# Two small expert groups of the second layer share their result tiles and scattering products; the first layer's small group scatters in two slices; three maxima over k stand earlier

## The chip, the cores and the metric

The kernel runs on one core of one Trainium2 chip. The time is device time in microseconds (us), from launch to end, and less is better. The engines are TensorE (PE; its weight loads are shown as PEld), VectorE (DVE), ScalarE (ACT), GpSimd (POOL) and SyncE (SP), which issues nearly all DMA transfers. Each engine works through its own instructions in the order in which they were written.

## The reference

Linear attention over 4 batches of 8 heads (576 tokens, 64 features a head), then two mixture-of-experts layers over the 2304 tokens of 512 features:

```python
q_s = exp(q - q.max(-1)); q_s /= q_s.sum(-1) + 1e-9
k_s = exp(k - k.max(2));  k_s /= k_s.sum(2) + 1e-9      # over the tokens
x = einsum('bhsd,bhde->bhse', q_s, einsum('bhsd,bhse->bhde', k_s, v))
...
# first layer: the best of 8 experts for each token, by order of arrival up to a capacity
h = relu(disp @ w1); y = h @ w2                           # 512 -> 1024 -> 512
out[i] = gate_w[i] * y[expert_idx[i], pos[i]]             # 0 where no place is left
# second layer: only tokens with x @ w_skip > 0
out[do_compute] = xc + gate_w * (relu(xc @ w1[e]) @ w2[e])
```

## The kernel before

**Layout.** x stands transposed in SBUF, 512 features as 4 chunks c of 128 partitions, 576 tokens along the free axis, one tile for each batch. A product over tokens is written in two halves of 288 columns.

**Large groups.** `COURSE` lists five large groups (layer, batch): (0,0), (0,1), (0,2), (1,0), (1,1). Each runs one expert over all 576 tokens of a batch, in 16 slices: 8 for the first weight matrix (L842), 8 for the second (L863), with 24 products of 288 columns in each slice. An fp32 operand is split into a high and a low part: `split_w` makes `wh` on ACT and `wl` on DVE (L784, L785), two slices ahead of use, and the slice's result in PSUM (`pair`) is evacuated as `hh` on ACT (L876) and `hl` on DVE (L877).

**The order.** Everything else is hung onto the slices by hand. One line of `COURSE` is one slice: its products, then `split_w` of the slice two ahead, then the words left of the bar, then `evacuate`, then the words right of the bar. Names with c, d, e, f, g, i are half batches of attention (`km`, `kt`, `kc`, `ke`, `kv`, ... are steps of k; `qm`, `q1`, ..., `qt` of q; `re` gives x). `km` takes the maximum of k over the tokens within each partition, three DVE operations (L378 to L380, tile `m`). `kt` transposes that on PE (L386, tile `pt`), so PE waits there for `km`. C and M are steps of the routing, O stores, G steps of the gate row, L and N loads of weights, X splits of x.

**Small groups.** An expert with at most 32 tokens of a batch is done apart: S is (0,2) with one such expert, T is (1,2) with two. The tokens are gathered (`g`), five steps `t` run the expert on 32 places (L1206), and its result in PSUM has four row blocks of 32 partitions: blocks 0 and 1 hold feature chunks 0 and 1, blocks 2 and 3 hold chunks 2 and 3, each pair of blocks the two partial sums over the hidden features. Step 4 splits that into the two tiles `y2` (high and low, L1223, L1224); their other places stay zero. `v` (`places`) compares each token's code with the 32 place codes, four copies side by side (L1228, L1232), and `a` (`place`) transposes that into `pT` (128 rows, 576 tokens). `u` (`put`, L1255 and L1259) scatters: for each chunk and token half two products of `y2[:, c]` with `pT` into a PSUM tile `pts`, and one DVE addition of it to x. Before, `put(t, i)` handles chunks 2i and 2i+1 of expert t: 8 products and 4 additions.

**PSUM.** All the small PSUM tiles (`pts`, `pt`, `ptl`, `px`, `pg`, `pgm`, `pkT`, ...) rotate through the three buffers of one pool, `bank`:

```python
pa = ctx.enter_context(tc.tile_pool(name="pa", bufs=3, space=bass.MemoryType.PSUM))
def bank(name):
    return pa.tile([P, 512], F32, name=name, tag="a")
```

The fourth such tile in a row therefore waits until the first has been read.

Of the kernel before, what the change touches and what calls it, by code (L numbers as in the profile page):

```python
# [9 lines left out]
F32 = mybir.dt.float32  # L10
# [3 lines left out]
ALU = mybir.AluOpType  # L14
# [3 lines left out]
P = 128  # L18
NJ = 5
LAST = 64  # L20
HT = 288
TINY = 32
# [25 lines left out]
    L5 c.q2 | C0.2 c.kc  # L48
    C0.3 c.ke d.qm |
    L6 C0.4 c.q3 | c.kv  # L50
    C0.5 c.qn d.q1 |
    L7 d.km | c.qt d.kt
    C0.6 d.q2 | d.kc
    d.ke | c.re G.0
    d.q3 X0 | d.kv
# [5 lines left out]
    C1.3 e.qm N3 f.ld | C1.4  # L61
    """),
    ((0, 1), """
    L4 C1.5 |
    e.km e.q1 | e.kt
    L5 C1.6 e.q2 | G.3 e.kc
    e.ke f.qm | G.1
    L6 e.q3 | e.kv
    e.qn f.q1 | G.2
    L7 f.km | e.qt f.kt  # L70
    f.q2 | f.kc
    f.ke | e.re
    f.q3 X0 | f.kv
# [20 lines left out]
    N2 g.qn S.v0 | S.t03  # L94
    X2 | S.a0 g.qt
    N3 | S.t04
    X3 | S.u00 S.u01
    """),
    ((1, 0), """
    L4 G.3 | g.rw  # L100
    g.rx | M2.1
    L5 | M2.2 M1.1
    M2.3 | M2.4
# [14 lines left out]
    L4 G.3 | T.t03 O0.2  # L118
    | T.a0 i.rw
    L5 i.rx | T.t04 C3.1  # L120
    T.v1 | T.t10 T.u00
    L6 | T.u01 C3.2 G.1
    C3.3 | T.t11 C3.4 O0.3
    L7 C3.5 G.2 | T.t12 T.a1
    | T.t13
    Z B |
    | T.t14
    | T.u10
    | T.u11 O1.0
    | O2.0  # L130
    | O1.1 O2.1
    | O2.2
# [6 lines left out]
def kernel(  # L139
# [17 lines left out]
    nc = tc.nc  # L157
    B, H, S, D = q.shape
# [23 lines left out]
    def bank(name):  # L182
        return pa.tile([P, 512], F32, name=name, tag="a")

    def long_bank(name):

        return pb.tile([P, 512], F32, name=name, tag="b")
# [17 lines left out]
    def tokens(a):  # L205
        return slice(a * HT, (a + 1) * HT)
# [7 lines left out]
    iota = c32[:, C_IOTA:C_IOTA + TINY]  # L214
# [9 lines left out]
    for i, g in enumerate((w_gate, w_gate2)):  # L224
        t = cp.tile([P, NC, 32], F32, name=f"wg{i}")
        nc.gpsimd.memset(t, 0.0)
        with nc.allow_non_contiguous_dma(reason="gate weights are small"):
            nc.scalar.dma_start(out=t[:, :, 0:E], in_=g.rearrange("(c p) e -> p c e", p=P))
            if i == 1:
                nc.scalar.dma_start(  # L230
                    out=t[:, :, E:E + 1], in_=w_skip.rearrange("(c p o) -> p c o", p=P, o=1)
# [22 lines left out]
    for i in range(2):  # L254
        t = cp.tile([P, 2, P], F32, name=f"kvd{i}")
# [694 lines left out]
    with tc.tile_pool(name="fp", bufs=1) as fp:  # L950
# [3 lines left out]
        a, b = [Half(0, hh, X[0], fp, 1) for hh in range(2)]  # L954
# [158 lines left out]
    hp = ctx.enter_context(tc.tile_pool(name="hp", bufs=1, reuse_waits="tile"))  # L1113
    hp = ctx.enter_context(tc.tile_pool(name="hp", bufs=1, reuse_waits="tile"))
# [7 lines left out]
    class Small:  # L1122
# [69 lines left out]
        def expert(self, t, step):  # L1192
            if step == 0:
                self.ph = long_bank("ph")
            elif step == 3:
                self.ph = long_bank("py")
            if step != 2:
                for i in {0: (0, 1), 1: (2, 3), 3: (4, 5), 4: (6, 7)}[step]:
                    w = self.tw.pop(8 * t + i)
                    for g in range(4):  # L1200
                        if i < 4:
                            lhsT, rhs = self.xs[:, i, 32 * t:32 * t + 32], w[:, 256 * g:256 * g + 256]
                        else:
                            lhsT = self.hT[:, g % 2, 32 * (i - 4):32 * (i - 4) + 32]
                            rhs = w.rearrange("p (u d) -> p u d", u=2)[:, g % 2, 256 * (g // 2):256 * (g // 2) + 256]
                        nc.tensor.matmul(  # L1206
                            out=self.ph[32 * g:32 * g + 32, :256], lhsT=lhsT, rhs=rhs, start=(i % 4 == 0), stop=(i % 4 == 3)
                        )
                    self.load(8 * t + i + 3)
            if step == 1:  # L1210
                self.h1 = hp.tile([P, 256], F32, name="h1", tag="h1")
                nc.scalar.activation(self.h1, self.ph[:, :256], AF.Relu)
            elif step == 2:
                pt = bank("pth")
                for u in range(2):
                    nc.tensor.transpose(pt[:, u * P:(u + 1) * P], self.h1[:, u * P:(u + 1) * P], ident)
                self.hT = hp.tile([P, 2, P], F32, name="hT", tag="h1")
                nc.vector.tensor_copy(out=self.hT, in_=pt[:, :2 * P].rearrange("p (u s) -> p u s", u=2))
            elif step == 4:
                for i in range(2):  # L1220
                    sl, cs = slice(64 * i, 64 * i + 64), slice(2 * i, 2 * i + 2)
                    src = self.ph[sl, :256].rearrange("p (c d) -> p c d", c=2)
                    nc.scalar.copy(y2[0][sl, cs], src)  # L1223
                    nc.vector.tensor_sub(y2[1][sl, cs], src, y2[0][sl, cs].bitcast(F32))  # L1224

        def places(self, t):
            cs = hp.tile([P, TINY], F32, name="cs2", tag="cs2")
            nc.vector.tensor_scalar(out=cs, in0=iota, scalar1=self.r["tlo"][:, t:t + 1], scalar2=None, op0=ALU.add)  # L1228
            self.p4 = hp.tile([P, NJ, 4, TINY], F32, name="p4", tag="ot", bufs=3)
            bb = [P, NJ, TINY]  # L1230
            for g in range(4):
                nc.vector.tensor_tensor(  # L1232
                    out=self.p4[:, :, g],
                    in0=self.r["z"].unsqueeze(2).to_broadcast(bb),
                    in1=cs.unsqueeze(1).to_broadcast(bb),
                    op=ALU.is_equal,
                )

# [8 lines left out]
            nc.tensor.transpose(pt[:, 0:LAST], p4f[:LAST, 4], ident[:LAST, :LAST])  # L1247
            nc.scalar.copy(pT[:, 4 * P:S], pt[:, 0:LAST])

        def put(self, t, i):  # L1250
            for c in (2 * i, 2 * i + 1):
                for a in range(2):
                    pt = bank("pts")
                    for n, u in enumerate(y2):
                        nc.tensor.matmul(  # L1255
                            out=pt[:, :HT], lhsT=u[:, c], rhs=self.pT[t][:, tokens(a)], start=(n == 0), stop=(n == 1)
                        )
                    x = self.x[:, c, tokens(a)]
                    nc.vector.tensor_add(x, x, pt[:, :HT])  # L1259
# [83 lines left out]
    for kk, (_, plan) in enumerate(COURSE):  # L1343
        lines = plan.strip().split("\n")
        assert len(lines) == NS
        for i, line in enumerate(lines):
            before, _, after = line.partition("|")
            groups[kk].products(i)
            n = NS * kk + i + 2
# [131 lines left out]
```

## Time and profile before

| What | Value |
|---|---|
| three timed runs | 416.24, 416.97, 419.02 us; median 416.97 |
| the profiled execution's own time | 416.55 us |
| its span, first to last instruction | 414.7 us |
| mean granted TensorE clock | 0.995 of full |
| PE busy | 393.7 us (95%) |
| DVE busy | 251.6 us (61%) |
| ACT busy | 182.3 us (44%) |
| POOL busy | 12.4 us (3%) |

Busy shares are of the span. Between the profiled execution's time and its span lie 1.85 us that the trace does not show. A timeline row names a start, a duration, the engine, the line, the operation with its tiles and shapes and a count of merged instructions; in square brackets stands how long the engine was idle before it and what ended that. Products overlap on PE, so the distance between two starts, not the duration, is what one costs.

### The profile page before, as it was taken

To read this page: it belongs to the slowest core of one execution; us is meant where nothing else is said; L and a number is where in the kernel's file an instruction comes from. 1 tells how busy PE (TensorE), PEld (TensorE's weight loads), DVE (VectorE), ACT (ScalarE), POOL (GpSimd) and SP (SyncE) were. 2 spreads that over 40 slices of the span, in tenths; PEclk is the share of its full clock that TensorE was granted. 3 is DMA by queue.
4 is the path that set the end of the run, shared out by engine and by line. 5 is a ranking of instruction groups with operands and counts; after the bars stand their busy time and mean duration, and the time that the engine had idled before them with its cause. 6 is when DMAs were issued, how large, how long until landed. Compare 5 with 4: busy or idle time off the path is not lost.

```text
span 414.7 us, 8456 instructions
## 1 busy us (share of the span) xinstructions
PE 393.7 (95%) x3241; PEld 351.1 (85%) x3241; DVE 251.6 (61%) x640; ACT 182.3 (44%) x547; POOL 12.4 (3%) x46
## 2 busy tenths in 40 slices
PE   8989898999999999999999999999999999899892
PEld 4656797898999989799999888899998988799881
DVE  4874789463586846278546656367777736654432
ACT  1656675734357772324346622333375342331211
POOL 2400000000000000000000100000000000000000
PEclk9999999999999999999999999999999999999998
DMA  8829926100970400293355771116315556363133
GB/s 207 220 54 262 255 72 193 31 2 2 295 182 9 124 2 2 82 300 96 107 195 178 217 216 52 51 52 232 101 53 183 182 180 214 92 204 123 31 101 102
DMA packets 72535, 54.48 MB, mean 131 GB/s; under 512 B 18454, under 2 KB 67114, under 8 KB 72490
## 3 DMA queue, kind: packets, MB, share of 16 engines
q1 hardware_dynamic: 70536, 53.60, 44.4%
q10 hardware_dynamic: 1954, 0.31, 0.6%
q8 instruction: 26, 0.43, 0.4%
q14 instruction: 19, 0.16, 0.1%
HBM read 49.16 MB, written 4.73 MB: 130 GB/s over the span
## 4 chain that ended last, share of the span: by engine, by line
PE 85%; DVE 8%; ACT 3%; issue 2%; DVEq 0%; ACTq 0%
PE pair L863 31%; PE pair L842 25%; PE pair L535 3%; PE px L495 3%; PE pxs L1150 2%; PE pk L437 2%; PE pl L596 2%; PE pto L1284 2%; PE ph L1206 1%; PE py L1206 1%; PE pts L1255 1%; PE pk L992 1%; PE ptq L463 1%; DVE hl L877 1%; PE pair L822 1%
## 5 line engine op out<-in xcount | busy, mean ns | idle before, releaser
L863 PE MATMUL pair<-hh,wh 128*128 128x288 f32 x320 | 98.3, 307 | 0.0
L863 PE MATMUL pair<-hh,wl 128*128 128x288 f32 x320 | 94.6, 296 | 0.0
L863 PE MATMUL pair<-hl,wh 128*128 128x288 f32 x320 | 94.5, 295 | 0.0
L842 PE MATMUL pair<-xh,wh 128*128 128x288 f32 x304 | 92.8, 305 | 0.0
L842 PE MATMUL pair<-xl,wh 128*128 128x288 f32 x304 | 89.6, 295 | 0.0
L842 PE MATMUL pair<-xh,wl 128*128 128x288 f32 x304 | 89.5, 295 | 0.0
L785 DVE TENSOR_TENSOR wl<-ws,wh 128x512 fp32r<-128x512 f32 x80 | 54.9, 686 | 35.9 <-ACT wh L784 35.4
L863 PEld LDWEIGHTS pair<-hh,wh 128*128 128x128 f32 x320 | 60.5, 189 | 3.8 <-issue 2.6
L863 PEld LDWEIGHTS pair<-hl,wh 128*128 128x128 f32 x320 | 60.7, 190 | 0.1
L876 ACT ACTIVATE hh<-pair 128x576 fp32r<-128x576 f32 x40 | 25.8, 645 | 79.2 <-PE pair L842 77.4
L863 PEld LDWEIGHTS pair<-hh,wl 128*128 128x128 f32 x320 | 60.5, 189 | 0.0
L842 PEld LDWEIGHTS pair<-xh,wh 128*128 128x128 f32 x304 | 57.1, 188 | 2.2 <-issue 0.9
L842 PEld LDWEIGHTS pair<-xl,wh 128*128 128x128 f32 x304 | 57.2, 188 | 0.1
L842 PEld LDWEIGHTS pair<-xh,wl 128*128 128x128 f32 x304 | 57.1, 188 | 0.0
L877 DVE SCALAR_TENSOR_TENSOR hl<-pair,hh 128x576 fp32r<-128x576 f32 x40 | 30.2, 755 | 37.1 <-ACT hh L876 37.1
L784 ACT CAST wh<-ws 128x512 fp32r<-128x512 f32 x80 | 49.3, 620 | 2.2 <-DMA ws<-in_moe_w_dram 1.5
L334 ACT ACTIVATE eq<-qt,mx 128x64 f32<-128x64 f32 x140 | 46.7, 338 | 0.5 <-DVE mx L323 0.5
L334 ACT ACTIVATION_READ_ACCUMULATOR eq<-qt,mx 128x1 f32 x140 | 26.6, 190 | 0.0
L535 PE MATMUL pair<-warm 128*128 128x384 f16 x94 | 18.7, 346 | 1.6 <-DVE warm L952 1.6
L785 DVE TENSOR_TENSOR xl<-x,xh 128x576 fp32r<-128x576 f32 x20 | 14.9, 752 | 6.0 <-ACT xh L784 6.0
L1285 ACT COPY ot<-pto 128x256 f32<-128x256 f32 (+1 forms) x24 | 7.0, 315 | 26.0 <-PE pto L1284 26.0
L535 PEld LDWEIGHTS <-warm 128*128 128x128 f16 x94 | 9.3, 104 | 8.1 <-issue 2.1
(210 smaller groups left out, 500.2 us busy)
## 6 DMA issues: line engine op xcount, KB each, us to landing
ws<-in_moe_w_dram SPq DMA_DIRECT2D x39, 512.0 KB, 4.7
tw<-in_moe_w_dram SPq DMA_DIRECT2D x24, 512.0 KB, 4.6
kt<-in_k_dram SPq DMA_DIRECT2D x8, 512.0 KB, 7.5
qt<-in_q_dram SPq DMA_DIRECT2D x8, 512.0 KB, 6.5
out_dram<-ot SPq DMA_DIRECT2D x12, 256.0 KB, 2.7
vt<-in_v_dram SPq DMA_DIRECT2D x16, 128.0 KB, 4.8
vt<-in_v_dram SPq DMA_DIRECT2D x3, 512.0 KB
mg<-gate SPq DMA_DIRECT2D x4, 288.0 KB, 7.2
```

The costliest lines, as they stand in the source:

```text
L334: nc.scalar.activation(self.eqv[:, h, j], self.qt[:, h, j], AF.Exp, bias=self.mx[:, i:i + 1], accum_out=self.qz[:, i:i + 1])
L437: nc.tensor.matmul(out=pk[64 * g:64 * g + 64, c * D1 + o:c * D1 + o + n], lhsT=self.kt[:rows(j), 2 * c + g, j], rhs=ones32[:rows(j), 0:1] ...
L495: nc.tensor.matmul(out=pt, lhsT=self.kd[:, c], rhs=self.qT[:, c, 0:4 * P], start=True, stop=True)
L535: nc.tensor.matmul(out=pw[:, 0, :3 * P], lhsT=warm16[:, 0:P], rhs=warm16, start=True, stop=True)
L596: nc.tensor.matmul(out=pl[32 * c:32 * c + 32, :HT], lhsT=self.weights[:, c], rhs=self.chunk(c, tokens(a)), start=True, stop=True,)
L784: nc.scalar.copy(hi, src)
L785: nc.vector.tensor_tensor(out=lo, in0=src, in1=hi.bitcast(F32), op=ALU.subtract)
L842: nc.tensor.matmul(out=self.pt[:, a, :HT], lhsT=u[:, c], rhs=w[:, c, tokens(a)], start=(c == 0 and n == 0), stop=(c == NC - 1 and n == 2),)
L863: nc.tensor.matmul(out=self.pt[:, a, :HT], lhsT=p_[:, f], rhs=w[:, tokens(a)], start=(v == 0 and f == 0 and n == 0), stop=(v == 1 and f == ...
L876: nc.scalar.activation(halves(hh), src, AF.Relu)
L877: nc.vector.scalar_tensor_tensor(out=halves(hl), in0=src, scalar=0.0, in1=halves(hh).bitcast(F32), op0=ALU.max, op1=ALU.subtract,)
L1150: nc.tensor.matmul(out=self.px[:, c * self.w:(c + 1) * self.w], lhsT=self.xt[:rows(j), c * P:(c + 1) * P], rhs=self.pj[:rows(j), j], start ...
```

## The change

- T's second expert writes its result's row blocks in the order 2, 3, 0, 1, so that its chunks 0 and 1 come to stand in rows 64 to 127 and its chunks 2 and 3 in rows 0 to 63. These are the places of `y2` that the first expert leaves free. `pT` number t holds the places of expert t in its rows 0 to 63 and those of the other in rows 64 to 127. One `put(i)` then scatters chunks 2i and 2i+1 of both experts. `T.u00` and `T.u01`, in slices 3 and 4 of (1,1), are gone; `T.u0` and `T.u1` stand where `T.u10` and `T.u11` stood.
- `places` makes the codes of both experts each time (two operations on `cs2` for T where there was one).
- S keeps its 16 products: `S.u0` stays at the end of (0,2), the last words of its last slice, and `S.u1` moves one slice on, to the first slice of (1,0), ahead of `g.rw`.
- `d.km`, `e.km` and `f.km` move from the left of the bar of one slice to the right of the bar of the slice before.

```diff
-    C0.5 c.qn d.q1 |
-    L7 d.km | c.qt d.kt
+    C0.5 c.qn d.q1 | d.km
+    L7 | c.qt d.kt
...
-    L4 C1.5 |
-    e.km e.q1 | e.kt
+    L4 C1.5 | e.km
+    e.q1 | e.kt
...
-    e.qn f.q1 | G.2
-    L7 f.km | e.qt f.kt
+    e.qn f.q1 | G.2 f.km
+    L7 | e.qt f.kt
...
-    X3 | S.u00 S.u01
+    X3 | S.u0
     """),
     ((1, 0), """
-    L4 G.3 | g.rw
+    L4 G.3 | S.u1 g.rw
...
-    T.v1 | T.t10 T.u00
-    L6 | T.u01 C3.2 G.1
+    T.v1 | T.t10
+    L6 | C3.2 G.1
...
-    | T.u10
-    | T.u11 O1.0
+    | T.u0
+    | T.u1 O1.0
...
+                        o = 32 * (g ^ 2 if t and i >= 4 else g)
...
-                            out=self.ph[32 * g:32 * g + 32, :256], lhsT=lhsT, rhs=rhs, start=(i % 4 == 0), stop=(i % 4 == 3)
+                            out=self.ph[o:o + 32, :256], lhsT=lhsT, rhs=rhs, start=(i % 4 == 0), stop=(i % 4 == 3)
...
-                    sl, cs = slice(64 * i, 64 * i + 64), slice(2 * i, 2 * i + 2)
+                    o = 64 * (i ^ t)
+                    sl, cs = slice(o, o + 64), slice(2 * i, 2 * i + 2)
...
-            cs = hp.tile([P, TINY], F32, name="cs2", tag="cs2")
-            nc.vector.tensor_scalar(out=cs, in0=iota, scalar1=self.r["tlo"][:, t:t + 1], scalar2=None, op0=ALU.add)
+            cs = hp.tile([P, 2, TINY], F32, name="cs2", tag="cs2")
+            for u in range(self.n):
+                nc.vector.tensor_scalar(
+                    out=cs[:, u], in0=iota, scalar1=self.r["tlo"][:, u:u + 1], scalar2=None, op0=ALU.add
+                )
...
-                    in1=cs.unsqueeze(1).to_broadcast(bb),
+                    in1=cs[:, (g // 2) ^ t if self.n == 2 else 0].unsqueeze(1).to_broadcast(bb),
...
-        def put(self, t, i):
+        def put(self, i):
+            pT = self.pT[i if self.n == 2 else 0]
             for c in (2 * i, 2 * i + 1):
...
-                            out=pt[:, :HT], lhsT=u[:, c], rhs=self.pT[t][:, tokens(a)], start=(n == 0), stop=(n == 1)
+                            out=pt[:, :HT], lhsT=u[:, c], rhs=pT[:, tokens(a)], start=(n == 0), stop=(n == 1)
```

Where the instructions stand, engine by engine (the first words of a row are the line and the operation, then out<-in and the shape; lines behind L1200 are numbered 3 to 7 higher in the changed kernel). First DVE in slices 5 and 6 of (0,0), at `d.km`; - is before, + is now:

```order
 L367 TENSOR_TENSOR eq<-eq,qz 128x4x5x64
 L877 SCALAR_TENSOR_TENSOR hl<-pair_83,hh 128x576
-L785 TENSOR_TENSOR wl_206<-ws_198,wh_202 128x512
-L378 TENSOR_TENSOR m_959<-kt 128x512
-L379 TENSOR_TENSOR m_960<-m_959 128x256
-L380 TENSOR_TENSOR m_960<-m_960,kt 128x256
+L378 TENSOR_TENSOR m_932<-kt 128x512
+L379 TENSOR_TENSOR m_933<-m_932 128x256
+L380 TENSOR_TENSOR m_933<-m_933,kt 128x256
+L785 TENSOR_TENSOR wl_206<-ws_198,wh_202 128x512
 L877 SCALAR_TENSOR_TENSOR hl<-pair_84,hh 128x576
 L388 TENSOR_REDUCE cm<-pt 128x2
```

The three operations of `km` changed places with one `wl` and nothing else; at `e.km` and `f.km` the same happens. Next DVE at the seam of (0,2) and (1,0), with S's additions (L1259, in the changed kernel L1266); before:

```order
L892 TENSOR_TENSOR x_123<-pair_83,mg 128x576
L1259 TENSOR_TENSOR x_123<-x_123,pts 128x288 x8
L785 TENSOR_TENSOR wl_208<-ws_199,wh_204 128x512
L909 TENSOR_SCALAR hi<-dlo_164 128x1
L910 SCALAR_TENSOR_TENSOR gm<-z_162,dlo_164,gw_163 128x5
L913 SCALAR_TENSOR_TENSOR gm<-z_162,hi,gm 128x5
L877 SCALAR_TENSOR_TENSOR hl<-pair_84,hh 128x576
L785 TENSOR_TENSOR wl_209<-ws_199,wh_205 128x512
```

and now:

```order
L892 TENSOR_TENSOR x_123<-pair_83,mg 128x576
L1266 TENSOR_TENSOR x_123<-x_123,pts 128x288 x4
L785 TENSOR_TENSOR wl_208<-ws_199,wh_204 128x512
L909 TENSOR_SCALAR hi<-dlo_164 128x1
L910 SCALAR_TENSOR_TENSOR gm<-z_162,dlo_164,gw_163 128x5
L913 SCALAR_TENSOR_TENSOR gm<-z_162,hi,gm 128x5
L877 SCALAR_TENSOR_TENSOR hl<-pair_84,hh 128x576
L1266 TENSOR_TENSOR x_123<-x_123,pts 128x288 x4
L785 TENSOR_TENSOR wl_209<-ws_199,wh_205 128x512
```

Four of S's eight additions now stand behind the evacuation `hl` of the first slice of (1,0). Last DVE in slices 3 and 4 of (1,1), where T's first expert was scattered; before:

```order
L1228 TENSOR_SCALAR cs_4241<-c_85,tlo_183 128x32
L1232 TENSOR_TENSOR p_4243<-z_180,cs_4241 128x5x32 x4
L877 SCALAR_TENSOR_TENSOR hl<-pair_83,hh 128x576
L1259 TENSOR_TENSOR x_123<-x_123,pts 128x288 x4
L785 TENSOR_TENSOR wl_208<-ws_201,wh_204 128x512
L877 SCALAR_TENSOR_TENSOR hl<-pair_84,hh 128x576
L1259 TENSOR_TENSOR x_123<-x_123,pts 128x288 x4
L611 TENSOR_REDUCE L<-ptl 128x64
```

and now:

```order
L1232 TENSOR_SCALAR cs_4242<-c_85,tlo_183 128x32 x2
L1238 TENSOR_TENSOR p_4245<-z_180,cs_4242 128x5x32 x4
L877 SCALAR_TENSOR_TENSOR hl<-pair_83,hh 128x576
L785 TENSOR_TENSOR wl_208<-ws_201,wh_204 128x512
L877 SCALAR_TENSOR_TENSOR hl<-pair_84,hh 128x576
L611 TENSOR_REDUCE L<-ptl 128x64
```

Eight additions are gone here and one `cs` operation came in; on PE the 16 products of `T.u00` and `T.u01` are gone between the same neighbours.

## Rows read from the trace of the kernel before

**Rows 1.** The page: busy time of PE, and the chain that ended last by engine.

```profile
PE 393.7 (95%) x3241; PEld 351.1 (85%) x3241; DVE 251.6 (61%) x640; ACT 182.3 (44%) x547; POOL 12.4 (3%) x46
PE 85%; DVE 8%; ACT 3%; issue 2%; DVEq 0%; ACTq 0%
```

**Rows 2.** Timeline of PE at the seam of (0,2) and (1,0), with S's 16 products.

```profile
253.38 0.95 PE L1255 MATMUL pts<-pT,y 128*128 128x288 f32 x6
254.75 2.04 PE L1255 MATMUL pts<-pT,y 128*128 128x288 f32 x10 [0.42 <-DVE x L1259]
256.63 0.30 PE L842 MATMUL pair<-xh,wh 128*128 128x288 f32 x1
...
259.81 0.38 PE L512 MATMUL pkT<-c,kvd 128*128 128x128 f32 x2
```

**Rows 3.** Timeline of PE in slices 3 and 4 of (1,1): T.u00 and T.u01.

```profile
347.92 1.62 PE L1255 MATMUL pts<-pT,y 128*128 128x288 f32 x8
349.38 0.29 PE L842 MATMUL pair<-xh,wh 128*128 128x288 f32 x1
...
352.55 0.96 PE L1255 MATMUL pts<-pT,y 128*128 128x288 f32 x6
354.61 0.53 PE L1255 MATMUL pts<-pT,y 128*128 128x288 f32 x2 [1.10 <-DVE x L1259]
354.97 0.66 PE L608 MATMUL ptl<-c,lp 128*128 128x128 f32 x4
```

**Rows 4.** Timelines of ACT and DVE around T.u01.

```profile
352.75 0.65 ACT L876 ACTIVATE hh<-pair 128x576 fp32r<-128x576 f32 x1 [4.57 <-PE pair L842]
...
353.44 0.76 DVE L877 SCALAR_TENSOR_TENSOR hl<-pair,hh 128x576 fp32r<-128x576 f32 x1 [2.79 <-ACT hh L876]
354.11 1.54 DVE L1259 TENSOR_TENSOR x<-x,pts 128x288 f32<-128x288 f32 x4
```

**Rows 5.** Timeline of PE: the transposes of d.kt, e.kt and f.kt.

```profile
71.13 0.41 PE L386 MATMUL pt<-c,m 128*128 128x128 f32 x2 [1.64 <-DVE m L380]
...
121.06 0.41 PE L386 MATMUL pt<-c,m 128*128 128x128 f32 x2 [0.63 <-DVE m L380]
...
141.75 0.41 PE L386 MATMUL pt<-c,m 128*128 128x128 f32 x2 [0.57 <-DVE m L380]
```

**Rows 6.** Timeline of DVE at f.km.

```profile
139.34 0.68 DVE L785 TENSOR_TENSOR wl<-ws,wh 128x512 fp32r<-128x512 f32 x1
139.94 0.68 DVE L378 TENSOR_TENSOR m<-kt 128x512 f32<-128x512 f32 x1
```

**Rows 7.** Timelines of ACT and PE behind d.kt, in slice 8 of (0,0).

```profile
79.75 1.05 ACT L502 COPY x<-px 128x512 f32<-128x512 f32 x2
...
80.37 1.52 PE L936 MATMUL pg<-c,gm 128*128 128x128 f32 x10
```

**Rows 8.** Timelines of DVE and PE behind e.kt, in slice 3 of (0,1).

```profile
127.74 0.23 DVE L913 SCALAR_TENSOR_TENSOR gm<-z,hi,gm 128x5 f32<-128x5 f32 x1
...
128.12 0.27 PE L918 MATMUL pgm<-c,gm 128*5 128x128 f32 x1
```

**Rows 9.** Timeline of ACT behind f.kt, in slice 7 of (0,1).

```profile
145.39 0.65 ACT L876 ACTIVATE hh<-pair 128x576 fp32r<-128x576 f32 x1 [0.70 <-PE pair L842]
```

**Rows 10.** DMA issues from 347.3 to 347.9 us, and PE's step T.t11 that uses it.

```profile
tw<-in_moe_w_dram SPq DMA_DIRECT2D x1, 512.0 KB, 3.6
...
359.08 1.07 PE L1206 MATMUL ph<-tw,xs 128*32 128x256 f32 x16
```

**Rows 11.** Windows around waits: start:end, length, busy us (count) by engine, granted clock, DMA.

```profile
69.00:75.00 6.00, 4.36 (x34) 4.11 (x33) 5.18 (x16) 3.38 (x14) 0.14 (x1) 1.00 0.71 178
346.00:358.00 12.00, 10.88 (x87) 9.37 (x86) 8.39 (x25) 2.31 (x4) 0.00 (x0) 1.00 0.48 157
```

**Rows 12.** Timeline of DVE in slice 3 of (1,1): T.v1 and the evacuation behind it.

```profile
345.81 0.23 DVE L1228 TENSOR_SCALAR cs<-c,tlo 128x32 f32<-128x32 f32 x1
...
347.71 0.76 DVE L877 SCALAR_TENSOR_TENSOR hl<-pair,hh 128x576 fp32r<-128x576 f32 x1 [0.60 <-ACT hh L876]
```

## The prediction

> **What bounds the kernel now.** I read the page first: PE is busy for 95% of the span and makes up 85% of the chain that ended last [rows 1]. In such a kernel work taken off PE comes out of the time one for one, as long as nothing else is late at that place, and a wait of PE comes out only as far as the next engine that PE meets is not late too. So I then went through PE's timeline for every idle time that the change touches, and behind each of them through the timelines of DVE and ACT to the next point where PE needs something from them. There are three kinds of place: the scattering of T in (1,1) [rows 3], that of S at the seam of (0,2) and (1,0) [rows 2], and the three transposes that wait for the maxima over k [rows 5].
>
> **T's scattering.** Of 32 products 16 go, and with them 8 additions. T.u00 takes PE from 347.92 to the next slice's first product at 349.38: 1.46 us. T.u01 takes it from 352.55 to the routing transposes at 354.97: 2.42 us, in which PE stood still for 1.10 because the fourth tile needs the buffer that the first addition frees [rows 3], and that addition is behind hh and hl on ACT and DVE [rows 4]. Both are on PE's path with nothing beside them: 1.46 + 2.42 = 3.88 us gone. Is something else late there once PE comes earlier? ACT's hh waits for PE's pair, and DVE's hl for hh [rows 4], so both move with PE. The step T.t11 at 359.08 needs weights that are asked for when T.t10 frees their buffer, issued between 347.3 and 347.9 and landing 3.6 us later, by 351.5 [rows 10]; in the changed kernel PE is there at 359.08 - 3.88 = 355.2, so 3.7 us are left. I take the whole 3.88. What T.u0 and T.u1 cost at the end is as before, since they have the counts, the neighbours and the wait of T.u10 and T.u11. The reversed row blocks of the second expert's second half change neither a count nor the turn through four blocks; 32 products of 32 columns in two steps are concerned, and 16 of them take 1.07 us [rows 10], 0.067 each. If the new order undid their overlap, the nearest row is a full-width product: 24 of them from 256.63 to 259.81, 0.1325 each [rows 2], so 32 x (0.1325 - 0.067) = 2.1 us. I take 0, and 2.1 is the bound. The additional cs operation for each of T.v0 and T.v1 is 0.23 us on DVE, which was idle for 0.60 before the evacuation that follows [rows 12]: nothing.
>
> **S's scattering.** The 16 products are kept, and only their place changes. Before they hold PE from 253.38 to 256.63, 3.25 us, with one short wait of 0.42, because the additions start at once and keep up [rows 2]. Cut in two, S.u0 needs six products up to the wait, two more from 254.75 on, thus until 254.75 + 2 x 0.1325 = 255.01: 1.63 us. S.u1 comes straight behind the 24 products of the first slice of (1,0), and its additions stand on DVE behind that slice's hl. Row for row that is what T.u01 was: 2.42 us until the next tile of the pool, here pkT, may start [rows 3, 4]. The bounds for S.u1 are its bare products, 8 x 0.1325 = 1.06, and T.u01's 2.42; T.u00's 1.46 had an expert step in front that gave hl its time, which S.u1 lacks. I take 2.42, the row with the same neighbours. So S costs 1.63 + 2.42 - 3.25 = +0.80 us: at this place the change makes PE wait longer. Queued behind S.u1 are pkT on PE, its copy on ACT and the next wl on DVE, and the users of the last two are a slice or more away.
> The Trainium skill, "Perfetto Trace Analysis", section "Matmuls", has independent groups of products rotate through PSUM banks, so that evacuating one overlaps the products of the next. Read as fulfilled with three buffers, S.u1 would cost its bare 1.06 and the sum below would come to 411.5; the 1.10 us that PE waits in T.u01 [rows 3] speaks against that reading.
>
> **The maxima over k.** km changes places with one wl on DVE, so m is ready earlier by the distance of the two starts, 139.94 - 139.34 = 0.60 us [rows 6]. PE's waits for m are 1.64, 0.63 and 0.57 [rows 5]; taken alone each gives 0.60, 0.60 and 0.57 back, 1.77 together. But DVE and ACT around them do the same work in the same time as before, so I looked for where PE meets them next. Behind d.kt, pg in slice 8 takes the buffer of the first px tile, and the first of the two copies from it, which start at 79.75 and take 1.05 for both, ends at about 79.75 + 0.55 = 80.30; PE starts pg at 80.37 [rows 7]. These copies stand behind exponentials on ACT that wait for DVE, not for PE. So PE would come 0.60 earlier and wait there: nothing is left of d. Behind e.kt, pgm in slice 3 reads gm, whose last operation ends at 127.74 + 0.23 = 127.97, and PE starts pgm at 128.12 [rows 8]; DVE comes to gm from ACT's exponentials, not from PE. PE gains at most 0.1 there. Behind f.kt it is otherwise: hh of the next slice had waited 0.70 for PE's pair [rows 9], so ACT, and DVE behind it, move with PE, and 0.57 stays. I take 0.60 for the three, with bounds of 0 and 1.77. The wl that now comes 1.6 us later is used two slices on, with 24 products of 3.18 us each between [rows 2]: nothing.
>
> **The sum**, in the profiled execution's own time: 416.55 - 3.88 + 0.80 - 0.60 = 412.87 us, a gain of 3.68 or 0.88%. The median of the runs shown lies 0.42 above that execution; 416.97 - 3.68 = 413.29. I name 413.1, between the two. About 1%, 4.17 us, is what a measurement of this kernel can tell from no change, and the forecast lies just inside it.
>
> **Rivals.** (A) The gains at d and e stay as well, because the copies and gm come earlier than the rows let me think. Then 416.55 - 3.88 - 1.77 + 0.80 = 411.7, faster by 1.2%. Against it: both are tied to DVE work that does not move. Chance 0.15. (B) Part of T's gain becomes another wait or loses its overlap. The largest price I find is the row blocks' 2.1 us: 412.87 + 2.1 = 415.0, no change. For it: it is not shown in the trace. Against it: the turn through the four blocks is kept. Chance 0.12. (C) Slower: TensorE's clock falls behind the new wait at S.u1. At present the granted clock is 1.00, the 2.4 GHz level, in the windows around waits of 1.64 and of 1.10 us [rows 11], so a wait of the same size should leave it there. If it did fall to the 1.2 GHz level for a stretch like the second of these windows, with 10.88 us of PE work in 12, that work would take 10.9 us more: 412.87 + 10.9 = 423.8. It decides from 3.7 us of PE work at the lower level on. Chance 0.03.
> The Trainium skill, "TensorE: Matmul & The Clock Gate", section "A second HAM failure mode: psum-queue depth-cycling", describes this: a kernel whose PE idles briefly and often while it cycles through PSUM banks has its clock go back and forth between the levels. By that rule C would be the outcome; the granted clock of 1.00 around three-buffer waits [rows 11] does not bear it out here.
>
> **How the numbers follow.** The forecast has 0.70. Its own spread is about 412.0 to 414.3: S.u1 between its bounds and a run's scatter. A point in the middle lies 0.3 us from the limit of 1%, so of its 0.70 I give 0.26 to faster and 0.44 to within 1%. With A to faster, B to within and C to slower, plus 0.01 for scatter, that is 0.41, 0.55 and 0.04. The range goes down to 411.4, under A, and up to 415.0, B; C and what lies beyond are left out.
>
> **What would show it.** In the changed kernel's trace: 32 pts products in place of 48; no idle time of PE and no late tw at T.t11; a wait of about 1.1 to 1.3 us at the fourth tile of S.u1 and 2.4 us from its first product to pkT; PE's waits for m about 1.0 at d and none at e and f, with new waits of about 0.5 before pg and pgm; and the granted clock unchanged at the seam. The prediction is wrong if PE is late at T.t11 or T.t14, if S.u1 takes much less than 2.4 us, if the waits at pg and pgm do not appear, or if the two steps with reversed row blocks take more than 1.07 us.

## The result

| | before | changed |
|---|---|---|
| median of five runs | 417.52 us (416.24 to 419.02) | 413.30 us (412.86 to 413.71) |
| ratio to before, 95% interval | | 0.9905 (0.9882 to 0.9928) |
| the profiled execution's own time | 416.55 us | 413.30 us |
| its span | 414.7 us | 411.4 us |
| PE busy | 393.7 us | 391.8 us |
| DVE busy | 251.6 us | 248.8 us |
| mean granted clock | 0.995 | 0.997 |

The kernel became faster by 0.95%, just inside the 1% that was taken as the limit; the interval reaches to both sides of that limit. The forecast was 413.1. The kernel before, timed again beside the experiments, had medians of 416.97 and 417.02 us. Against these the 413.30 is a gain of 3.7 us, 0.9%; the 417.52 of the table makes it look like 4.2.

For finer readings than the times allow I measure on PE's timeline between two marks that every kernel here has: the start of c.kt's transposes (the wait for m at 46.90 before, 47.62 after) and the start of the last output transposes (408.00 before, 405.13 after). Between them lie 361.10 us before and 357.51 after: 3.59 less. The rows of the marks, before and then changed (the changed kernel's first mark heads the next fence):

```profile
46.90 0.41 PE L386 MATMUL pt<-c,m 128*128 128x128 f32 x2 [0.55 <-DVE m L380]
408.00 0.49 PE L1284 MATMUL pto<-c,x 128*64 128x128 f32 x3 [0.79 <-DVE x L900]
...
405.13 0.49 PE L1291 MATMUL pto<-c,x 128*64 128x128 f32 x3 [0.80 <-DVE x L900]
```

The span differs by 3.3, because the stretch ahead of the first mark was 0.72 longer in this execution and that behind the last one 0.4 shorter, and neither holds anything that was changed. One trace of each kernel stands behind each distance. Where two kernels have the same work, the distances agree closely: from PE's wait at 170 us to the first wait in S lie 84.46 us in the kernel before, and 84.48 and 84.47 in the two experiments below that scatter S in one piece.

PE's waits of the changed kernel, from its timeline, those of the maxima and of what comes behind them (they answer to [rows 5], [rows 7] and [rows 8]; the last row is f.kt, with no bracket and so no wait):

```profile
47.62 0.41 PE L386 MATMUL pt<-c,m 128*128 128x128 f32 x2 [0.55 <-DVE m L380]
...
71.25 0.41 PE L386 MATMUL pt<-c,m 128*128 128x128 f32 x2 [1.03 <-DVE m L380]
...
81.06 1.52 PE L936 MATMUL pg<-c,gm 128*128 128x128 f32 x10 [0.50 <-ACT x L502]
...
128.82 0.27 PE L918 MATMUL pgm<-c,gm 128*5 128x128 f32 x1 [0.45 <-DVE gm L913]
...
141.85 0.41 PE L386 MATMUL pt<-c,m 128*128 128x128 f32 x2
```

At d the wait went from 1.64 to 1.03, which is the 0.60 that was forecast; 10 us later PE stands 0.50 before pg, and behind that it is 0.69 later than before (81.06 against 80.37) where the first mark was 0.72 later: 0.03 is left of 0.60. At e the wait of 0.63 is gone, and 0.45 came in before pgm. At f the wait is gone, and nothing came in its place up to the next wait of PE, at 170.38 (170.29 before): f.kt starts only 0.10 later than before, and of the 0.72 by which this execution started later, 0.63 is made up by 170.

The seam of (0,2) and (1,0) on PE's timeline, with S in two pieces (it answers to [rows 2]):

```profile
253.49 0.95 PE L1262 MATMUL pts<-pT,y 128*128 128x288 f32 x6
254.86 0.53 PE L1262 MATMUL pts<-pT,y 128*128 128x288 f32 x2 [0.42 <-DVE x L1266]
255.23 0.30 PE L842 MATMUL pair<-xh,wh 128*128 128x288 f32 x1
...
258.41 0.95 PE L1262 MATMUL pts<-pT,y 128*128 128x288 f32 x6
260.46 0.53 PE L1262 MATMUL pts<-pT,y 128*128 128x288 f32 x2 [1.11 <-DVE x L1266]
260.83 0.44 PE L512 MATMUL pkT<-c,kvd 128*128 128x128 f32 x2
```

S.u0 takes 1.74 us, S.u1 2.42, together 4.16 where one piece took 3.25. On DVE S.u1's additions come behind hl, as those of T.u01 did [rows 4]:

```profile
259.29 0.76 DVE L877 SCALAR_TENSOR_TENSOR hl<-pair,hh 128x576 fp32r<-128x576 f32 x1 [2.33 <-ACT hh L876]
259.96 1.53 DVE L1266 TENSOR_TENSOR x<-x,pts 128x288 f32<-128x288 f32 x4
```

In (1,1) PE goes straight on where T.u00 and T.u01 stood (it answers to [rows 3] and [rows 10]; L1208 is L1206 of the kernel before). T.t11, at 356.20, has no bracket and so no wait, and the second expert's two steps with reversed row blocks, at 366.10 and 373.65, take what the others take. The wait at the fourth tile of T.u1 stays:

```profile
347.99 1.07 PE L1208 MATMUL ph<-tw,xs 128*32 128x256 f32 x16
348.99 0.40 PE L842 MATMUL pair<-xh,wh 128*128 128x288 f32 x1
...
356.20 1.07 PE L1208 MATMUL ph<-tw,xs 128*32 128x256 f32 x16
...
366.10 1.07 PE L1208 MATMUL py<-tw,hT 128*32 128x256 f32 x16
...
373.65 1.07 PE L1208 MATMUL py<-tw,hT 128*32 128x256 f32 x16
...
377.94 1.50 PE L1262 MATMUL pts<-pT,y 128*128 128x288 f32 x8
...
384.64 0.53 PE L1262 MATMUL pts<-pT,y 128*128 128x288 f32 x2 [1.22 <-DVE x L1266]
```

The kernel before, at the first and the last of these places:

```profile
346.92 1.07 PE L1206 MATMUL ph<-tw,xs 128*32 128x256 f32 x16
...
387.52 0.54 PE L1255 MATMUL pts<-pT,y 128*128 128x288 f32 x2 [1.21 <-DVE x L1259]
```

The windows of the seam and of the first slices of (1,1), with the granted clock behind the counts:

```profile
252.00:262.00 10.00, 8.47 (x62) 7.94 (x61) 6.82 (x17) 2.64 (x6) 0.00 (x0) 1.00 0.19 54
346.00:358.00 12.00, 12.00 (x120) 10.42 (x118) 7.04 (x20) 3.59 (x7) 0.00 (x0) 1.00 0.58 184
```

PE is busy for all of the 12 us from 346 to 358, where before it was for 10.88 [rows 11]: no wait came in behind T's removal. The clock stays at 1.00, the 2.4 GHz level, through the new wait at the seam.

### The profile page after: what moved, and what is told of

It reads as the page before. It is cut to its first block, busy times and chain, and to the rows that moved or that the text cites. A ratio compares the mean times of both kernels' runs of the same rounds, so it can differ in the third digit from the quotient of the medians.

```text
span 411.4 us, 8415 instructions
## 1 busy us (share of the span) xinstructions
PE 391.8 (95%) x3225; PEld 349.2 (85%) x3225; DVE 248.8 (60%) x634; ACT 182.3 (44%) x547; POOL 12.8 (3%) x46
## 4 chain that ended last, share of the span: by engine, by line
PE 74%; ACT 3%; DVE 2%; issue 1%; ACTq 0%; DVEq 0%
PE pair L863 31%; PE pair L842 23%; PE pxs L1150 2%; PE pk L437 2%; PE pl L596 2%; PE pto L1291 2%; PE ph L1208 1%; PE py L1208 1%; ACT eq L334 1%; PE ptq L463 1%; PE px L495 1%; PE ptx L1165 1%; PE pts L1262 1%; PE ptl L608 1%; ACT hh L876 1%
## 5 line engine op out<-in xcount | busy, mean ns | idle before, releaser
L535 PE MATMUL pair<-warm 128*128 128x384 f16 x94 | 19.6, 358 | 1.6 <-DVE warm L952 1.6
```

What stands on the lines that cost most here:

```text
L535: nc.tensor.matmul(out=pw[:, 0, :3 * P], lhsT=warm16[:, 0:P], rhs=warm16, start=True, stop=True)
```

## The experiments

Each experiment is an edit of the changed kernel; in the diffs - is the changed kernel and + the experiment. A ratio compares the time with that of the kernel before, as everywhere. "Marks" is the distance between the two marks above.

**T alone.** S in one piece and all three km back:

```diff
-    X3 | S.u0
+    X3 | S.u0 S.u1
-    L4 G.3 | S.u1 g.rw
+    L4 G.3 | g.rw
-    C0.5 c.qn d.q1 | d.km
-    L7 | c.qt d.kt
+    C0.5 c.qn d.q1 |
+    L7 d.km | c.qt d.kt
```

and the same for e.km and f.km.

> Only T's shared tiles and products are kept; S scatters in one piece and the three maxima stand where they stood before the change. Measured on PE's timeline from the start of c.kt's transposes to the start of the last output transposes, the kernel before takes 361.10 us and the changed one 357.51. My theory: T alone is worth 3.9 us, so 357.2, a little less than with the whole change, and a time of about 413.2. Rival: the split of S and the maxima are gains of their own; then T alone is worth less than the whole, 358.0 to 359.5. No wait of PE in S longer than 0.42, waits for m of 1.64, 0.63 and 0.57 as before.

Measured: marks 404.00 - 46.80 = 357.20, 412.91 us, ratio 0.9906 (0.9891 to 0.9921). The sharing of T's products is worth 361.10 - 357.20 = 3.90 us and is the whole gain of the change and a little more; the other two parts together cost 0.3. So together they are no gain; what each does by itself the next two experiments show.

**S in one piece.** The first two of those edits alone.

> The changed kernel with S's scattering back in one piece at the end of (0,2). My theory: the split costs 0.9 us (1.74 + 2.42 against 3.25), so the distance between the two marks falls from 357.51 to 356.6 and the time to about 412.4. Rival: the split frees DVE at the seam and is neutral or a gain; then 357.5 or more.

Measured: marks 403.91 - 47.37 = 356.54, 0.97 less than the changed kernel; 412.26 us, ratio 0.9891 (0.9876 to 0.9906). The split costs what the rows of the seam say (0.91, and 0.05 for the transposes pkT, which take longer directly behind S.u1), and as it stands in the changed kernel it is a loss. PE's timeline has the old pattern again:

```profile
254.63 2.04 PE L1262 MATMUL pts<-pT,y 128*128 128x288 f32 x10 [0.42 <-DVE x L1266]
```

**All three maxima back.**

> The changed kernel with the three maxima back where they were. My theory: together they are worth 0.6 us, so the distance between the marks rises from 357.51 to 358.1; the waits for m are 1.64, 0.63 and 0.57 again and those before pg and pgm (0.50, 0.45) are gone. Rival: each keeps its own 0.6; then 359.2 to 359.3.

Measured: marks 405.46 - 47.25 = 358.21, 0.70 more than the changed kernel; 413.92 us, ratio 0.9929 (0.9916 to 0.9943). The waits for m are 1.63, 0.62 and 0.59, and no wait stands before pg or pgm. The maxima are a gain of their own, as the rival of the first experiment had it, but three moves of 0.60 each are worth little more than one.

**Only f.km moved.** d.km and e.km back.

> The changed kernel with only f.km moved; d.km and e.km stand where they stood before. My theory: d and e gave nothing, so the distance between the marks (c.kt's transposes to the last output transposes) stays at 357.5 with the waits 1.64 and 0.63 back, none at f, and none before pg and pgm. Rival: f alone is not what carries the 0.6, since each move counts; then 357.9 or more.

Measured: marks 404.42 - 46.85 = 357.57, 0.06 from the changed kernel; 413.29 us, ratio 0.9921 (0.9901 to 0.9941). f alone carries the whole 0.6 to 0.7; d and e carry nothing.

**The gate's products one slice later.** If the gain of d is lost at pg and nowhere else, it must come back when pg stands where its buffer is long free:

```diff
-    d.ke | c.re G.0
-    d.q3 X0 | d.kv
+    d.ke | c.re
+    G.0 d.q3 X0 | d.kv
```

> The changed kernel with G.0, whose pg waits 0.50 for the buffer of px, put one slice later, behind the 24 products of slice 9 of (0,0), where the copies from px are long done. My theory: the gain of d.km then stays, and the distance between the marks falls from 357.51 to 357.0 (0.50 less), if mg, now made later, does not hold up the evacuation of slice 9 for longer than the pair is free. Rival: the wait moves to another place behind d (pk, or mg in front of the evacuation) and 357.5 stays.

Measured: marks 404.24 - 47.63 = 356.61, 0.90 less than the changed kernel, where 0.50 was expected; 412.64 us, ratio 0.9893 (0.9877 to 0.9910). The mechanism holds, since the wait before pg is gone and no other came. Of the other 0.4 the larger part is no wait that the traces show. PE's timeline of this kernel:

```profile
80.03 0.55 PE L489 MATMUL px<-qT,kvd 128*128 128x64 f32 x4
80.39 0.38 PE L863 MATMUL pair<-hh,wh 128*128 128x288 f32 x1
...
83.65 1.41 PE L936 MATMUL pg<-c,gm 128*128 128x128 f32 x10
85.00 1.83 PE L437 MATMUL pk<-vt,kt 128*64 128x65 f32 x40
86.75 0.40 PE L863 MATMUL pair<-hh,wh 128*128 128x288 f32 x1
```

The same stretch, from the last px group to the first product behind pk, in the kernel before and then in the changed kernel, whose last row shows the copies on ACT that free the buffers:

```profile
79.89 0.55 PE L489 MATMUL px<-qT,kvd 128*128 128x64 f32 x4
...
86.95 0.40 PE L863 MATMUL pair<-hh,wh 128*128 128x288 f32 x1
...
80.01 0.56 PE L489 MATMUL px<-qT,kvd 128*128 128x64 f32 x4
...
82.51 0.40 PE L863 MATMUL pair<-hh,wh 128*128 128x288 f32 x1
...
85.89 1.83 PE L437 MATMUL pk<-vt,kt 128*64 128x65 f32 x40
87.65 0.40 PE L863 MATMUL pair<-hh,wh 128*128 128x288 f32 x1
...
80.44 1.05 ACT L502 COPY x<-px 128x512 f32<-128x512 f32 x2
```

It takes 7.64 us in the changed kernel, 7.06 in the kernel before, which has the same order on PE and no bracket at pg [rows 7], and 6.72 here. So the delay that came in at pg cost 0.58, a little more than its bracket of 0.50 and nearly the whole 0.60 of d. Behind that, 0.34 is left. The step from px to the group behind it takes 0.36 here and 0.48 before, and pg up to the next group 1.35 here and 1.45 in the changed kernel (81.06 to 82.51). The last 0.1 lies between the first product of the pair and the group behind the pair, which is pg here and was pk. The 0.12 at px can still be a wait: pg starts 0.62 behind the start of the copies in the kernel before (79.75 [rows 7] to 80.37) and in the changed one (80.44 to 81.06), so PE may have stood there briefly already before. The 0.2 of the other two steps come from the order of the groups on PE.

**The gate row's transpose one slice later.** The same at e: G.1 moves from slice 3 of (0,1) to slice 4, left of the bar, ahead of e.q3.

> The changed kernel with G.1, whose pgm waits 0.45 for gm, put one slice later in (0,1). My theory: the wait before pgm goes, but DVE and ACT are tied to their own chain up to f.km, so PE waits about 0.4 to 0.5 for m at f.kt and the distance between the marks stays at 357.5. Rival: the gain of e.km stays as that of f did; then 357.0 to 357.1 and no wait at f.

Measured: marks 405.56 - 48.03 = 357.53, as the changed kernel; 413.10 us, ratio 0.9910 (0.9894 to 0.9925). The wait before pgm is gone and comes back at f.kt:

```profile
142.27 0.41 PE L386 MATMUL pt<-c,m 128*128 128x128 f32 x2 [0.41 <-DVE m L380]
```

So from e to f DVE and ACT set the pace, and the place of pgm only decides where PE waits.

**Additions ahead of the evacuation.** Whether the wait at the fourth tile comes from the evacuation that DVE does first, or from additions that are too slow for three buffers, is told apart by changing nothing but their order on DVE:

```diff
-    L4 G.3 | S.u1 g.rw
+    L4 G.3 S.u1 | g.rw
-    | T.u1 O1.0
+    T.u1 | O1.0
```

> The changed kernel with S.u1 and T.u1 left of the bar: their products stay where they are on PE, their additions on DVE stand ahead of the slice's evacuation in place of behind it. My theory, the wait of PE at the fourth tile is the evacuation (hh on ACT, hl or the gated product on DVE) in front of the first addition: both waits (1.11 and 1.22) fall to 0.1 or less, S.u1 takes 1.3 to 1.5 us in place of 2.42 and T.u1 about the same in place of 2.54; the distance between the marks falls from 357.51 to 355.4, the time to about 411.2. Rival, the additions themselves are too slow for three buffers: the waits stay at about 0.4 or more and at most 1.3 us is gained; or the evacuations, now 1.5 us later, hold up the products that need the pair, and nothing is gained.

Measured: marks 402.78 - 47.49 = 355.29, 2.22 less than the changed kernel; 411.34 us, ratio 0.9869 (0.9854 to 0.9884). Both waits, 1.11 in S.u1 and 1.22 in T.u1, are gone, and each of the two pieces takes 1.34 us, where S.u1 took 2.42 and T.u1 2.54:

```profile
258.32 1.50 PE L1262 MATMUL pts<-pT,y 128*128 128x288 f32 x8
259.66 0.44 PE L512 MATMUL pkT<-c,kvd 128*128 128x128 f32 x2
...
381.32 1.50 PE L1262 MATMUL pts<-pT,y 128*128 128x288 f32 x8
382.66 1.20 PE L1291 MATMUL pto<-c,x 128*128 128x128 f32 x5
```

On DVE the additions now start with their own tile, and hl stands behind them without anybody waiting for it:

```profile
258.78 1.55 DVE L1266 TENSOR_TENSOR x<-x,pts 128x288 f32<-128x288 f32 x4 [1.91 <-PE pts L1262]
260.25 0.75 DVE L877 SCALAR_TENSOR_TENSOR hl<-pair,hh 128x576 fp32r<-128x576 f32 x1
```

Three buffers are enough here for additions that come at once; the rival falls.

**All that helped.** The additions first, G.0 one slice later, and S.u0 left of the bar too (`X3 S.u0 |`).

> Three edits to the changed kernel: additions of S.u1 and T.u1 ahead of the evacuation, G.0 one slice later, and S.u0 left of the bar too, so that its additions stand ahead of the evacuation of the last slice of (0,2). My theory: 355.29 with the first edit, 0.5 less for the second, and 0.4 less for the third (S.u0 1.34 in place of 1.74): 354.4 between the marks and a time of 410.2 to 410.5. Rival: the three meet another wait that takes the place of what they free; 355.0 or more.

Measured: marks 401.06 - 47.09 = 353.97; 409.73 us (409.51 to 410.82), ratio 0.9831 (0.9815 to 0.9846). That is 1.7% faster than the kernel before and the fastest version of this study. It is 0.4 below the expected distance, the same 0.4 as with G.0 alone. S.u0 takes 1.34 as well:

```profile
252.06 1.50 PE L1262 MATMUL pts<-pT,y 128*128 128x288 f32 x8
253.40 0.29 PE L842 MATMUL pair<-xh,wh 128*128 128x288 f32 x1
```

This turns the reading of the split. S in two pieces costs 1.74 + 2.42 = 4.16 us in the changed kernel, but 1.74 + 1.34 = 3.08 with S.u1's additions first and 1.34 + 1.34 = 2.68 here; the one piece cost 3.25. The loss thus came from the place of the additions and not from the split as such. One piece with its additions first was not run, so whether the split is worth anything by itself stays open.

## Why the prediction was right

- **T, forecast 3.88.** Right: from the step T.t10 to the last wait of T.u1 the distance fell from 387.52 - 346.92 = 40.60 to 384.64 - 347.99 = 36.65, by 3.95, and T alone gave 3.90 between the marks. That PE would not be late at the weights was right too: no wait at T.t11, nor from there to T.u1. The bound of 2.1 us for the row blocks did not come in, as the two steps take 1.07 each.
- **S, forecast +0.80.** Right in mechanism and sign, a little small: +0.91 by the rows of the seam, 0.97 by the experiment. S.u1 took the 2.42 of the row that was named for it, to the hundredth. The term that was off is S.u0, set at 1.63 and measured at 1.74: behind the wait the last two products need 0.37 to the next group (254.86 to 255.23), not two times 0.1325. That price was read from the products of the pair; the pts products in the same [rows 2] took 0.188 each (ten from 254.75 to 256.63). The lower bound for S.u1, 1.06, has the same flaw: without any wait the piece takes 1.34.
- **The maxima, forecast 0.60 of a possible 1.77.** Right point by point: 0.63 by the rows up to the wait at 170, 0.70 by taking all three back, and f alone gives it. The waits at pg (0.50) and at pgm (0.45) are where they were named. That these two places are the cause is shown for pg by moving it, which brought d's gain back (0.58), and for pgm by moving it, which sent the wait on to f. The 3.18 us that the prediction gives for 24 products is that of all 24 together.
- **The sum.** -3.95 + 0.98 - 0.63 = -3.60 between the marks, against the forecast -3.68. Here 0.98 is the whole stretch from the wait at 170 to the step T.t10, which holds S's 0.91. The misses are small and partly cancel: T and the maxima gave 0.10 more than forecast, S cost 0.18 more. That the ratio came out within 1% and not beyond is in part luck: the point forecast lay 0.3 us from that limit, and the measured interval reaches across it.
- **The rivals.** A, that d and e keep their gains, is refuted by the run with f alone. B is refuted by the window without a wait and the steps of 1.07. C, the clock, did not happen: the granted clock was 1.00, the 2.4 GHz level, through a wait of 1.11 us. The 3.7 us that C names would only undo the gain; to be slower by 1% the kernel would have had to lose about 8. The Trainium skill's "TensorE: Matmul & The Clock Gate", section "A second HAM failure mode: psum-queue depth-cycling", tells of a kernel whose PE, cycling through PSUM banks, was idle briefly and so often that its clock went back and forth; in the windows read here it did not move.
- **The rotation of the buffers.** By the Trainium skill's "Perfetto Trace Analysis", section "Matmuls", rotating banks let an evacuation overlap the next products. The three buffers do rotate, and S.u1 still waited 1.11; with the additions first on DVE it did not wait. So in this kernel the overlap came only once the additions, which free the buffer, had no evacuation in front of them on DVE.

What stays open is small: why the order px, pair, pg, pk takes 0.2 to 0.34 less on PE than px, pg, pair, pk, and how much of that is a wait without a bracket, and the stretches outside the marks, which differ by some tenths from one execution to the next.

## What to carry to other kernels

When an engine is full, count the work that leaves it, but for each wait that is taken away follow both engines to the next place where they meet: of three equal moves of 0.60 us two were lost there and one stayed. Work that is cut in two can pay the buffer wait in both pieces; ahead of cutting it, look at what stands in the consumer's queue in front of the operation that frees the buffer. Moving that operation ahead of an evacuation that PE did not need so soon was worth 2.2 us here for two words changed in a table, while the split, with its additions left behind the evacuation, cost 0.97. Of the 3.9 us that T's sharing brought, 1.10 was a wait of the same kind [rows 3]; whether moving T.u01's additions alone would have brought that back was not run.

## What was not expected of the hardware

The same ten products of pg took 1.45 us between px and products of the pair, and 1.35 between products of the pair and pk. With the step out of the pair, 0.1 shorter when pg came behind it and not pk, that made 0.2 us in which PE is not seen to wait. The order of small groups on PE was therefore worth some tenths here, even where nothing waits.
